# A three-stage attention and mixing kernel: unit 0's decays in two halves, and a new order of all steps

## The chip, the core and the metric

The kernel runs on one core of one Trainium2 chip. Its metric is the device time of one execution in microseconds (us): 578.5 us is the median of three runs of the kernel before (578.36 to 580.26). Five engines work side by side, each through its own list of instructions in order: TensorE (PE in the rows, PEld for its loads of weights), VectorE (DVE), ScalarE (ACT), GpSimd (POOL) and SyncE (SP). ACT, POOL and SP also issue DMAs.

## The reference

Three stages, for batch 4, 8 heads, 768 tokens, 48 channels a head (384 in all):

```python
# 1: linear attention with a decay per channel and token
for t in range(S):
    state = alpha[:, :, t, :, None] * state + np.einsum('bhd,bhe->bhde', k[:, :, t], v[:, :, t])
    y[:, :, t] = np.einsum('bhd,bhde->bhe', q[:, :, t], state)
...
# 2: mixing over tokens with a phase, then over channels
theta = x @ w_theta
zr, zi = x * np.cos(theta), x * np.sin(theta)
u = x + np.einsum('ts,bsd->btd', w_tok_r, zr) + np.einsum('ts,bsd->btd', w_tok_i, zi)
x = u + np.maximum(u @ w_ch, 0.0)
...
# 3: a gated layer with a second mixing over tokens
h = np.maximum(x @ w_in, 0.0)
u, v = h[..., :512], h[..., 512:]
v_n = (v - mu) / np.sqrt(var + 1e-06)
out = (u * (np.einsum('ts,bsd->btd', w_spatial, v_n) + b_spatial[None, :, None])) @ w_out
```

## The kernel before, in words

The work of stages 1 and 2 is cut into 24 units: 4 sequences of 6 blocks of 128 tokens. A unit u goes through these steps, named by the functions that issue them:

- `load_al`, `load_qk`, `load_v` (L360, L370, L375) load its decays, its queries and keys, and its values.
- `att_scan` (L380, L388, L391, VectorE) turns the decays into running products: a scan backward over 8 groups of 66 numbers, a reciprocal of 8 numbers, and a scan forward. `att_qk` (L414) multiplies queries and keys by them.
- TensorE takes over: `att_k` (L463) transposes keys, `att_u` (L480) makes the state's increments, `att_a` (L428) the scores, `att_y` (L527) the outputs; from unit 6 on one step, `att_uya` (L602), does most of this for two units. VectorE masks the scores (`att_mask`, L435) and carries the state on (`att_s`, L495, and `att_t`, L508).
- `tr_p` (L634), `th_p` (L674, L677) and ScalarE's and VectorE's steps between them make the phase; `z_m` (L716, L712 for unit 0), `z_h` (L720) and `z_l` (L724) the two products that are mixed over tokens; `tokmix` (L750) adds them into five banks of PSUM, which hold one sequence. After the sixth unit `evac` (L774) empties the banks and `ch_p` (L802) mixes channels.

Stage 3 (L926 to L1160) follows per sequence, its first products already beside the last units.

The weights come in 28 pieces, 22 of them packed. A packed piece is loaded by `raw_f64` (L247; GpSimd issues the first 16), unpacked by `top` (L253, ScalarE) and `join` (L262, VectorE), and split into two parts by `high` (L273, ScalarE) and `low` (L281, VectorE); unit 0's pair is multiplied whole before it is split. The raw pieces share 2 buffers, `top` and `join` share one tile (zeros), and the joined pieces one (f); a piece's load waits until the `join` two pieces earlier has read its buffer.

Fourteen products named `fill` (L761, 2 instructions each) multiply a tile of zeros into one of the five banks before the first `tokmix` adds to it. They need only the small tile of constants (`cst_sb`) and the zeroed tile `heads`, so they can stand anywhere ahead of it.

What sets the order: the functions declare about 1700 steps, and `ORDER`, a table of numbers written into the kernel, says in which order they are issued. Each engine gets its own instructions in that order and waits for others by semaphores. Tiles come from pools that go round: 2 buffers for decays (al), 3 for queries and keys (qk), 2 for values (vd). A load waits on its issuing engine until the step that read the buffer last is done, and what stands behind it on that engine waits too.

The constant AH decides on unit 0's decays. With AH = 0, `load_al` and `att_scan` handle all 8 groups of unit 0 at once. With AH = 1, `load_al` takes groups 0 to 3 and a further step `load_ah` (L365) groups 4 to 7, and `att_half` scans the first four before `att_scan` scans the others:

```python
n = 4 * SEG if AH and u == 0 else 8 * SEG
issuer("load_al", u).dma_start(t[:, :n], al_in[u, :, :n])
...
def att_half(u):
    scans(u, 0, 4, "bif")
...
def att_scan(u):
    if AH and u == 0:
        scans(u, 4, 8, "bif")
    else:
        scans(u, 0, 8, "f" if u in RP else "bif")
```

Of the kernel before, what the change touches and what calls it, by code (L numbers as in the profile page):

```python
# [75 lines left out]
AH = 0  # L76
# [13 lines left out]
1 130 167 177 131 67 0 175 7 132 178 176 179 133 180 68 134 69 181 12 138 139 70 140 8 71 135 141 9 214 142 215 10 2 165 137 188 136 13 185 11 143 14  # L90
186 217 187 17 144 182 145 172 146 170 189 168 183 3 169 190 184 251 191 192 252 148 4 216 174 218 253 5 37 173 171 193 164 6 18 222 225 149 254 223
147 166 150 194 151 219 195 19 196 224 152 22 198 255 155 153 197 154 260 220 38 199 156 163 261 39 200 256 221 42 40 226 159 201 23 258 227 41 202
289 229 228 257 161 24 259 263 25 27 292 290 157 291 230 204 43 262 231 26 162 232 233 264 203 44 160 265 77 45 234 327 266 328 15 205 235 28 46 236
206 301 267 29 237 158 293 32 268 30 207 78 269 31 271 212 270 238 273 79 239 272 80 47 330 298 20 208 299 240 294 241 213 33 296 295 16 81 297 300
274 302 209 329 275 34 210 276 72 303 242 277 35 211 331 364 243 402 48 304 336 244 332 337 36 279 338 278 333 247 49 335 280 50 52 249 334 281 339
305 51 73 340 250 366 306 282 365 341 307 74 287 401 308 310 75 57 311 367 309 248 53 312 342 76 313 314 245 343 403 54 474 315 344 317 368 62 246 316
345 318 55 288 347 346 319 56 369 348 58 370 371 372 320 285 404 325 373 349 374 286 59 350 351 375 82 63 405 283 352 353 376 21 409 437 60 323 377
410 61 354 378 355 64 284 438 379 411 406 439 356 412 324 407 83 413 357 473 321 408 440 380 326 381 65 384 382 383 322 66 385 441 358 386 414 387 445
476 360 390 446 388 415 389 391 361 475 416 477 546 359 92 447 442 448 444 417 443 362 418 1009 392 421 1008 419 363 420 393 422 400 481 1010 423 394
482 449 1011 509 450 398 424 427 1012 451 425 426 84 483 399 452 510 478 512 480 395 511 396 479 453 397 454 484 455 456 1013 485 545 486 513 457 428  # L100
517 1014 429 458 1015 518 430 459 460 433 1016 548 487 431 488 514 516 515 489 519 435 490 581 520 461 521 493 462 580 522 492 463 547 436 464 87 549
494 465 1017 491 466 495 553 1018 432 496 1019 583 497 434 554 499 523 550 498 584 467 582 524 1020 555 552 551 469 556 500 616 471 1021 525 472 526
527 528 588 557 468 615 589 501 558 502 470 559 585 587 586 529 590 618 617 507 651 652 530 1022 531 532 591 533 619 560 1026 561 562 563 534 1023 535
623 508 536 1027 564 537 625 624 538 1024 88 565 1025 503 566 1028 567 543 654 568 592 505 620 593 653 626 594 627 506 655 596 687 595 622 569 504 597
570 621 688 598 571 572 659 599 660 573 544 541 600 628 601 690 602 629 661 542 724 630 656 658 662 631 663 539 657 632 723 603 634 689 633 578 664
604 691 576 605 540 606 635 607 726 574 636 695 575 696 637 577 638 1030 639 665 640 1031 641 614 727 579 610 725 666 697 692 698 694 642 667 608 669
699 1032 643 759 795 611 668 1033 670 612 1034 671 693 613 700 733 644 672 731 673 649 732 674 677 701 675 609 728 702 730 729 703 734 645 705 760 704
676 707 706 761 735 736 794 762 1035 650 708 1036 1039 678 763 679 1037 709 680 710 647 1038 713 1040 711 767 797 648 712 768 737 714 646 764 796 715
769 766 738 683 1042 765 770 739 798 684 741 740 771 743 742 829 716 830 802 1041 744 803 719 745 746 681 747 832 749 772 685 773 866 799 831 804 801
774 800 686 775 833 776 865 748 778 777 1043 682 750 779 1046 780 751 781 805 752 1044 1047 837 1045 721 838 868 782 806 839 717 807 902 783 840 722  # L110
835 784 841 842 901 808 834 1048 867 809 869 785 757 1049 786 1050 787 836 873 812 718 811 904 720 813 755 814 874 815 753 810 816 817 843 818 819 756
870 844 875 872 820 871 845 876 754 847 877 846 903 821 937 849 848 938 878 790 905 850 909 851 758 788 852 853 940 854 855 791 910 879 1053 856 789
911 880 907 792 912 906 1052 881 793 882 883 913 828 857 973 885 884 908 1054 822 941 939 1055 974 886 824 858 887 888 945 976 823 946 891 826 825 977
827 914 947 915 85 86 89 861 975 916 943 93 105 859 948 942 90 949 917 944 1056 889 862 919 918 863 890 950 920 892 1061 91 893 106 1057 1062 94 107
921 111 894 108 864 1058 922 981 923 860 982 924 927 951 925 926 109 897 978 983 928 895 929 1059 952 930 979 898 1064 110 899 1060 102 1065 1063 896
980 953 900 955 954 112 956 957 103 113 933 984 114 104 935 985 97 958 986 959 960 931 961 962 1070 987 115 1103 1068 963 98 964 1071 1066 965 1069
966 988 1067 934 989 116 990 1072 936 991 117 992 932 993 1029 967 994 95 995 969 996 96 998 971 997 999 968 118 99 1000 972 125 1001 970 1106 119
1108 1002 1107 100 1006 1109 1004 101 1051 1003 120 1007 1073 1005 1075 1110 1074 1076 1085 1077 1117 1111 1086 1094 1112 121 1091 1095 1118 1113 1124
1114 1119 1115 1116 1120 1080 1092 1125 122 1100 1126 126 1078 1101 1127 1121 1098 1081 1122 123 1123 1089 1099 1082 1090 1079 124 1087 1128 1096 1088
1104 1131 1097 1105 1129 1083 1102 127 1084 1130 128 1138 1132 129 1133 1208 1218 1154 1139 1134 1093 1228 1140 1145 1135 1141 1136 1155 1137 1152  # L120
1142 1146 1143 1147 1168 1153 1144 1148 1149 1150 1161 1151 1219 1156 1220 1222 1189 1157 1158 1229 1162 1163 1232 1233 1196 1164 1165 1223 1166 1170
1169 1167 1234 1182 1171 1172 1177 1238 1197 1239 1159 1173 1174 1175 1209 1184 1240 1178 1179 1214 1241 1180 1176 1160 1242 1185 1181 1235 1191 1243
# [13 lines left out]
1586 1587 1662 1579 1636 1588 1580 1619 1589 1581 1582 1583 1642 1590 1584 1663 1591 1615 1592 1628 1593 1616 1620 1595 1594 1621 1651 1622 1623 1596  # L136
1624 1617 1629 1625 1671 1649 1618 1626 1627 1637 1630 1638 1639 1640 1653 1631 1643 1632 1641 1633 1644 1650 1655 1645 1652 1634 1660 1646 1647 1654
1648 1669 1661 1672 1656 1664 1657 1658 1678 1659 1665 1666 1676 1667 1668 1679 1683 1677 1670 1673 1680 1674 1686 1681 1675 1684 1682 1685 1689 1687
1688 1692 1690 1691 1695 1693 1694 1698 1696 1697 1699 1700
""".split()]  # L140


# [1487 lines left out]
```

## Time and profile before

| | |
|---|---|
| median of three runs | 578.5 us (578.36 to 580.26) |
| the profiled execution | 579.89 us, its span 578.1 us |
| TensorE busy | 561.8 us, 97% of the span |
| VectorE busy | 443.5 us, 77% |
| ScalarE busy | 253.1 us, 44% |
| bytes moved by DMA | 65.74 MB, mean 114 GB/s |

The span begins with the first instruction and ends with the last; 1.8 us of the execution lie around it. Matmuls are pipelined and the ends of their rows are modelled, so a row of TensorE can look busy while it waits. A row's duration overlaps the next row's start a little on VectorE as well, so what a step costs on a full engine is read from start to start. A row of several instructions is marked x and their number; "idle before" names what ended the wait.

### The profile page before, as it was taken

To read this page: it belongs to the slowest core of one execution; us is meant where nothing else is said; L and a number is where in the kernel's file an instruction comes from. 1 tells how busy PE (TensorE), PEld (TensorE's weight loads), DVE (VectorE), ACT (ScalarE), POOL (GpSimd) and SP (SyncE) were. 2 spreads that over 40 slices of the span, in tenths; PEclk is the share of its full clock that TensorE was granted. 3 is DMA by queue.
4 is the path that set the end of the run, shared out by engine and by line. 5 is a ranking of instruction groups with operands and counts; after the bars stand their busy time and mean duration, and the time that the engine had idled before them with its cause. 6 is when DMAs were issued, how large, how long until landed. Compare 5 with 4: busy or idle time off the path is not lost.

```text
span 578.1 us, 13520 instructions
## 1 busy us (share of the span) xinstructions
PE 561.8 (97%) x5765; PEld 518.0 (90%) x5765; DVE 443.5 (77%) x785; ACT 253.1 (44%) x474; POOL 27.2 (5%) x62
## 2 busy tenths in 40 slices
PE   4998999999999999999999999999999999999997
PEld 3866888899999999999999899998999999989997
DVE  7979999998788698789656877678666685577470
ACT  3576765435434444335465433344424341344122
POOL 1111100000000000000000110000000110001000
PEclk9999999999999999999999999999999999999999
DMA  7966774527343425424256343001103010201002
GB/s 259 336 223 227 245 242 141 169 69 238 105 135 100 130 58 176 128 88 112 87 161 203 140 146 128 1 0 42 42 1 101 23 42 1 96 28 41 1 1 82
DMA packets 27739, 65.74 MB, mean 114 GB/s; under 512 B 2976, under 2 KB 13856, under 8 KB 27424
## 3 DMA queue, kind: packets, MB, share of 16 engines
q1 hardware_dynamic: 25216, 52.65, 27.8%
q0 software_dynamic: 2176, 11.86, 6.0%
q8 instruction: 45, 0.74, 0.5%
q10 hardware_dynamic: 288, 0.37, 0.2%
q14 instruction: 14, 0.11, 0.1%
HBM read 52.68 MB, written 9.44 MB: 107 GB/s over the span
## 4 chain that ended last, share of the span: by engine, by line
PE 80%; DVE 8%; issue 2%; ACT 0%; DVEq 0%; ACTq 0%
PE acc L750 20%; PE acc L1079 11%; PE psv L938 9%; PE po L1137 9%; PE pu L1011 9%; PE psc L802 6%; PE psuya L602 5%; PE sp L1050 4%; PE th L674 3%; PE th L677 1%; DVE qk L414 1%; DVE al L380 1%; PE pst L634 1%; PE psk L463 1%; DVE wf L262 1%
## 5 line engine op out<-in xcount | busy, mean ns | idle before, releaser
L750 PE MATMUL acc<-w,zs 128*128 128x384 f32 (+2 forms) x828 | 164.3, 344 | 0.5 <-DVE zs L724 0.5
L750 PEld LDWEIGHTS acc<-w,zs 128*128 128x128 f32 x828 | 132.2, 188 | 12.6 <-DVE zs L724 0.8
L1011 PE MATMUL pu<-xs,w 128*128 128x384 f32 x288 | 53.3, 336 | 0.0
L938 PE MATMUL psv<-w,xs 128*128 128x512 f32 x216 | 52.9, 394 | 0.0
L1137 PE MATMUL po<-w,gs 128*128 128x384 f32 x288 | 52.3, 336 | 0.0
L1137 PEld LDWEIGHTS po<-w,gs 128*128 128x128 f32 x288 | 50.2, 188 | 1.0 <-ACT v L949 0.3
L1011 PEld LDWEIGHTS pu<-xs,w 128*128 128x128 f32 x288 | 50.3, 188 | 0.5 <-ACT o L1147 0.2
L938 PEld LDWEIGHTS psv<-w,xs 128*128 128x128 f32 x216 | 40.2, 187 | 8.4
L1123 ACT CAST gs<-t 128x384 fp32r<-128x384 f32 x32 | 16.3, 513 | 66.2 <-DVE t L1116 66.2
L802 PE MATMUL psc<-us,wch 128*128 128x384 f32 (+1 forms) x243 | 40.8, 319 | 0.1
L802 PEld LDWEIGHTS psc<-us,wch 128*128 128x128 f32 x243 | 38.2, 189 | 0.7 <-DVE xT L812 0.4
L380 DVE TENSOR_TENSOR_SCAN al<-al,heads 112x527 f32<-112x527 f32 x24 | 30.0, 1248 | 5.4 <-DMA al<-in_al 5.4
L674 PE MATMUL th<-wth,xh 128*128 128x384 f32 x144 | 30.1, 343 | 1.9 <-DVE tmp L508 1.9
L1079 PE MATMUL acc<-w,mx 128*128 128x384 f32 x162 | 30.9, 337 | 0.0
L1079 PE MATMUL acc<-wt,vns 128*128 128x384 f32 x162 | 30.8, 336 | 0.0
L391 DVE TENSOR_TENSOR_SCAN al<-al,heads 112x527 f32<-112x527 f32 x24 | 30.1, 1256 | 0.8
L414 DVE TENSOR_TENSOR qk<-qk,al 112x1024 f32<-112x1024 f32 x24 | 29.2, 1217 | 0.1
L681 ACT ACTIVATE kk<-th,magic 128x384 f32<-128x384 f32 x24 | 14.0, 582 | 34.6 <-PE th L677 34.6
L1079 PEld LDWEIGHTS acc<-w,mx 128*128 128x128 f32 x162 | 28.5, 188 | 0.0
L1079 PEld LDWEIGHTS acc<-wt,vns 128*128 128x128 f32 x162 | 28.5, 188 | 0.0
L674 PEld LDWEIGHTS th<-wth,xh 128*128 128x128 f32 x144 | 24.9, 188 | 3.9 <-issue 2.7
L720 ACT CAST zs<-z 128x768 fp32r<-128x768 f32 x23 | 19.2, 835 | 19.4 <-DVE z L716 19.4
(126 smaller groups left out, 1051.0 us busy)
## 6 DMA issues: line engine op xcount, KB each, us to landing
qk<-in_qk SPq DMA_DIRECT2D x24, 512.0 KB, 4.5
raw<-in_w POOLq DMA_DIRECT2D x14, 772.0 KB, 5.9
vd<-in_v SPq DMA_DIRECT2D x24, 288.0 KB, 3.6
al<-in_al SPq DMA_DIRECT2D x23, 264.0 KB, 3.3
raw<-in_w SPq DMA_DIRECT2D x6, 772.0 KB, 5.6
out<-o SPq DMA_DIRECT2D x24, 192.0 KB, 1.9
x2d<-xT SPq DMA_DIRECT2D x6, 576.0 KB, 4.4
ay<-ms SPq DMA_DIRECT2D x42, 64.0 KB, 3.3
```

Of the source, the lines that this page charges most:

```text
L380: nc.vector.tensor_tensor_scan(out=rt[:, :0:-1], data0=al[:, :0:-1], data1=one[:, :0:-1], initial=1.0, op0=ALU.mult, op1=ALU.add)
L391: nc.vector.tensor_tensor_scan(out=al[:, :n], data0=al[:, :n], data1=one[:, :n], initial=1.0, op0=ALU.mult, op1=ALU.add)
L414: nc.vector.tensor_tensor(out=x, in0=x, in1=st[u]["ar"], op=ALU.mult)
L602: i = nc.tensor.matmul(ps, w, v, start=start, stop=stop)
L674: nc.tensor.matmul(th, xh[:, 0, k], wth[:, pr, k], start=(k == 0 and pr == 0), stop=False)
L750: nc.tensor.matmul(acc[b, n][:, c0:c1], zs[:, pl, ri, m * 128:(m + 1) * 128], w[:, pr, t0:t1], start=first and n != 1, stop=last, skip_gro ...
L802: nc.tensor.matmul(ps, wch[:, pl, k, m * 128:(m + 1) * 128], us[:, pr, k], start=(n == 0), stop=(n == 3 * KD - 1),)
L938: nc.tensor.matmul(ps, xs2[:, pl, k, o:o + 128], win[pr, "v"][:, k], start=(n == 0), stop=(n == 3 * KD - 1),)
L1011: nc.tensor.matmul(pu, win[f // 2][:, pl, k * 256 + f % 2 * 128:k * 256 + f % 2 * 128 + 128], xq[b, h][:, pr, k], start=(n == 0), stop=(n ...
L1050: nc.tensor.matmul(sp[:, :TH], vns[b, s][:, pl, f * 128:(f + 1) * 128], wsp[s][:, pr, t], start=(n == 0), stop=(n == 3 * NS - 1),)
L1079: nc.tensor.matmul(g, left(b, n, j, pl, c), right(n, j, pr), start=(n in (1, 5, 6) and i == 0), stop=(i == 3 * NJ - 1), skip_group_check=n ...
L1137: nc.tensor.matmul(po, gs[b][:, pl, f, s * 128:(s + 1) * 128], wo[f // 2][:, pr, f % 2 * DM:(f % 2 + 1) * DM], start=(n == 0), stop=(n == ...
```

## The change

AH goes from 0 to 1, and the table `ORDER` is replaced. There are two new steps, `load_ah` and `att_half`, both for unit 0. The number of zero products (`FILL`) is fourteen in both kernels; their places differ.

```diff
-AH = 0
+AH = 1
...
 ORDER = [int(n) for n in """
-1 130 167 177 131 67 0 175 7 132 178 176 179 133 180 68 134 69 181 12 138 139 70 140 8 71 135 141 9 214 142 215 10 2 165 137 188 136 13 185 11 143 14
...
+1 130 0 133 67 7 131 132 179 180 181 134 173 177 135 167 165 68 136 171 176 69 140 178 141 182 12 70 142 137 8 143 183 216 217 71 187 144 188 9 189
...
```

The first place is the program's start, on VectorE. Before, the scans of units 0 and 1 (L380 to L391, 527 numbers a row each), then unit 0's `att_qk`, the first `join`, and unit 1's `att_qk`:

```order
L380 SCALAR_TENSOR_TENSOR al<-al,heads 112x527
L388 RECIPROCAL al<-al 112x8
L391 SCALAR_TENSOR_TENSOR al<-al,heads 112x527
L380 SCALAR_TENSOR_TENSOR al<-al,heads 112x527
L388 RECIPROCAL al<-al 112x8
L391 SCALAR_TENSOR_TENSOR al<-al,heads 112x527
L414 TENSOR_TENSOR qk<-qk,al 112x1024
L262 SCALAR_TENSOR_TENSOR wf<-raw,zeros 128x768
L414 TENSOR_TENSOR qk<-qk,al 112x1024
L281 SCALAR_TENSOR_TENSOR w<-wf,w 128x768
```

After, two scans of 263 numbers for unit 0, its `att_qk`, the first `join`, and only then unit 1's scan:

```order
L380 SCALAR_TENSOR_TENSOR al<-al,heads 112x263
L388 RECIPROCAL al<-al 112x4
L391 SCALAR_TENSOR_TENSOR al<-al,heads 112x263
L380 SCALAR_TENSOR_TENSOR al<-al,heads 112x263
L388 RECIPROCAL al<-al 112x4
L391 SCALAR_TENSOR_TENSOR al<-al,heads 112x263
L414 TENSOR_TENSOR qk<-qk,al 112x1024
L262 SCALAR_TENSOR_TENSOR wf<-raw,zeros 128x768
L380 SCALAR_TENSOR_TENSOR al<-al,heads 112x527
L388 RECIPROCAL al<-al 112x8
L391 SCALAR_TENSOR_TENSOR al<-al,heads 112x527
L495 TENSOR_TENSOR ss<-acc_152,al 112x192
```

Unit 0's `att_qk` has moved ahead of unit 1's scan, and the first `join` too. On SyncE the load of the second half stands behind that of the first; on ScalarE the load of unit 1's decays, which stood behind that of the constants, now stands behind the loading of the activation table and one activation (L1167). On TensorE the zero products ahead of unit 0's `att_k` are six instead of three.

The second place is what VectorE has between unit 2's second `att_s` (the first row shown), which frees the buffer that unit 4's decays are loaded into, and unit 4's scan (the last row). Before:

```order
L495 TENSOR_TENSOR ss<-tmp,al 112x192
L281 SCALAR_TENSOR_TENSOR w<-wf,w 128x768
L508 TENSOR_TENSOR tmp<-acc_415,ss 112x192
L435 TENSOR_TENSOR ms<-psa,cst_sb 128x256
L262 SCALAR_TENSOR_TENSOR wf<-raw,zeros 128x768
L495 TENSOR_TENSOR ss<-tmp,al 112x192
L380 SCALAR_TENSOR_TENSOR al<-al,heads 112x527
```

After:

```order
L495 TENSOR_TENSOR ss<-tmp,al 112x192
L435 TENSOR_TENSOR ms<-acc_368,cst_sb 128x256
L508 TENSOR_TENSOR tmp<-acc_438,ss 112x192
L262 SCALAR_TENSOR_TENSOR wf<-raw,zeros 128x768
L435 TENSOR_TENSOR ms<-psa,cst_sb 128x256
L691 SCALAR_TENSOR_TENSOR r<-kk,th 128x384
L435 TENSOR_TENSOR ms<-psa,cst_sb 128x256
L281 SCALAR_TENSOR_TENSOR w<-wf,w 128x768
L495 TENSOR_TENSOR ss<-tmp,al 112x192
L262 SCALAR_TENSOR_TENSOR wf<-raw,zeros 128x768
L380 SCALAR_TENSOR_TENSOR al<-al,heads 112x527
```

Four more rows stand between them now: two masks (L435), the second `join` (L262) and unit 1's L691; the two kernels have the same VectorE steps ahead of this scan but for `att_half`. On SyncE, around the same load, before (from unit 3's decays to unit 4's queries and keys):

```order
L360 DMA al<-in_al 128x528
L370 DMA qk<-in_qk 128x1024
L375 DMA vd<-in_v 128x576 x2
L360 DMA al<-in_al 128x528
L456 DMA ay<-ms 64x256 x2
L370 DMA qk<-in_qk 128x1024
```

and after (from unit 3's values to unit 4's values):

```order
L375 DMA vd<-in_v 128x576
L360 DMA al<-in_al 128x528
L370 DMA qk<-in_qk 128x1024
L375 DMA vd<-in_v 128x576
L370 DMA qk<-in_qk 128x1024
L360 DMA al<-in_al 128x528
L456 DMA ay<-ms 64x256 x2
L375 DMA vd<-in_v 128x576
```

Unit 3's values are now loaded ahead of unit 2's, and unit 4's queries and keys ahead of unit 4's decays and of the moves of unit 3's scores (L456).

The third place is on VectorE near unit 5's `z_l` (L724), the last unit of the first sequence. The scan in these rows is unit 8's, the L495 unit 7's second `att_s`. Before:

```order
L495 TENSOR_TENSOR ss<-tmp,al 112x192
L724 TENSOR_TENSOR zs<-z,zs 128x768
L380 SCALAR_TENSOR_TENSOR al<-al,heads 112x527
L388 RECIPROCAL al<-al 112x8
L391 SCALAR_TENSOR_TENSOR al<-al,heads 112x527
L659 TENSOR_TENSOR xh<-pst,xh 128x384
L281 SCALAR_TENSOR_TENSOR w<-wf,w 128x768
```

After:

```order
L380 SCALAR_TENSOR_TENSOR al<-al,heads 112x527
L388 RECIPROCAL al<-al 112x8
L391 SCALAR_TENSOR_TENSOR al<-al,heads 112x527
L495 TENSOR_TENSOR ss<-tmp,al 112x192
L659 TENSOR_TENSOR xh<-pst,xh 128x384
L281 SCALAR_TENSOR_TENSOR w<-wf,w 128x768
L724 TENSOR_TENSOR zs<-z,zs 128x768
```

The same seven rows stand in another order: the scan (L380 to L391), L659 and a `low` (L281) have moved ahead of the `z_l`. The rest of the program keeps its steps, in an order that differs in many places by a few steps.

## Rows read from the trace of the kernel before

**Rows 1.** The page: busy us, share of the span and instructions by engine
```profile
PE 561.8 (97%) x5765; PEld 518.0 (90%) x5765; DVE 443.5 (77%) x785; ACT 253.1 (44%) x474; POOL 27.2 (5%) x62
```

**Rows 2.** Three stretches: length, busy us (instructions) by engine, PEclk, DMA share, GB/s
```profile
4.16:41.54 37.38, 32.85 (x517) 26.12 (x518) 32.50 (x52) 20.09 (x36) 3.70 (x7) 1.00 0.80 278
41.54:103.00 61.46, 57.91 (x858) 48.81 (x857) 60.95 (x91) 39.41 (x71) 3.90 (x9) 1.00 0.64 213
103.00:575.00 472.00, 471.09 (x4393) 443.06 (x4391) 349.30 (x638) 192.09 (x367) 17.49 (x39) 1.00 0.27 88
```

**Rows 3.** VectorE's timeline, 4 to 18 us: start, us, line, operation, idle before
```profile
4.16 1.26 DVE L380 TENSOR_TENSOR_SCAN al<-al,heads 112x527 f32<-112x527 f32 x1 [2.49 <-DMA al<-in_al]
...
6.87 1.23 DVE L380 TENSOR_TENSOR_SCAN al<-al,heads 112x527 f32<-112x527 f32 x1
...
9.55 1.20 DVE L414 TENSOR_TENSOR qk<-qk,al 112x1024 f32<-112x1024 f32 x1
10.66 0.95 DVE L262 SCALAR_TENSOR_TENSOR wf<-raw,zeros 128x768 uint32<-128x768 uint32 x1
...
14.30 0.55 DVE L262 SCALAR_TENSOR_TENSOR wf<-raw,zeros 128x384 uint32<-128x384 uint32 x1
...
17.47 0.96 DVE L262 SCALAR_TENSOR_TENSOR wf<-raw,zeros 128x768 uint32<-128x768 uint32 x1 [0.67 <-ACT zeros L253]
```

**Rows 4.** VectorE's timeline again, 33 to 42 us
```profile
33.42 0.95 DVE L262 SCALAR_TENSOR_TENSOR wf<-raw,zeros 128x768 uint32<-128x768 uint32 x1
34.29 0.42 DVE L435 TENSOR_TENSOR ms<-acc,cst_sb 128x256 f32<-128x256 f32 x1
...
34.89 0.55 DVE L691 SCALAR_TENSOR_TENSOR r<-kk,th 128x384 f32<-128x384 f32 x1
...
35.68 0.35 DVE L495 TENSOR_TENSOR ss<-tmp,al 112x192 f32<-112x192 f32 x1
...
38.28 0.35 DVE L495 TENSOR_TENSOR ss<-tmp,al 112x192 f32<-112x192 f32 x1
41.54 1.25 DVE L380 TENSOR_TENSOR_SCAN al<-al,heads 112x527 f32<-112x527 f32 x1 [2.90 <-DMA al<-in_al]
```

**Rows 5.** DMAs in flight near 1.2 us: count, KB each, us to landing
```profile
raw<-in_w POOLq DMA_DIRECT2D x1, 772.0 KB, 7.7
qk<-in_qk SPq DMA_DIRECT2D x1, 512.0 KB, 4.6
al<-in_al SPq DMA_DIRECT2D x1, 264.0 KB, 3.3
al<-in_al ACTq DMA_DIRECT2D x1, 264.0 KB, 4.9
cst_sb<-in_cst ACTq DMA_DIRECT2D x1, 96.0 KB, 3.5
```

**Rows 6.** The same view, the one load of decays near 36 us
```profile
al<-in_al SPq DMA_DIRECT2D x1, 264.0 KB, 5.5
```

**Rows 7.** The page's list of DMA issues, the stored outputs
```profile
out<-o SPq DMA_DIRECT2D x24, 192.0 KB, 1.9
```

**Rows 8.** ScalarE's timeline, the first 10 us
```profile
1.67 1.28 ACT L1167 ACT_TABLE_LOAD   x1 [1.67 <-PEq L1619]
...
9.23 1.06 ACT L253 ACTIVATE zeros<-raw 128x768 f16<-128x768 bf16 x1 [6.07 <-DMA raw<-in_w]
```

**Rows 9.** GpSimd's timeline, near 35 us
```profile
34.67 0.53 POOL L247 DMA_DIRECT2D raw<-in_w  x1 [3.61 <-DVE wf L262]
```

**Rows 10.** TensorE's timeline, three places in the first 100 us
```profile
4.39 2.90 PE L761 MATMUL acc<-heads,cst_sb 112*128 112x256 f32 x6 [4.39 <-DMA cst_sb<-in_cst]
21.32 1.89 PE L761 MATMUL acc<-heads,cst_sb 112*128 112x256 f32 x8
97.10 1.08 PE L750 MATMUL acc<-w,zs 128*128 128x512 f32 x5
```

**Rows 11.** VectorE's timeline, near 92 us
```profile
92.01 0.95 DVE L724 TENSOR_TENSOR zs<-z,zs 128x768 fp32r<-128x768 f32 x1
```

98 rows, old and new, of the table ORDER are left out of this document.

## The prediction

> **What bounds the kernel now.** I read the page's busy shares first: TensorE is busy for 97% of the span [rows 1], so a gain must come from the little time in which it is not. The windows say where that is [rows 2]. From 103 to 575 us TensorE is busy 471.09 of 472.00 us, and nothing is to be had there. From 4.16 to 41.54 us it misses 4.5 us, and to 103 us another 3.6. Before 4.16 us nothing runs on it.
>
> The second number to read in those windows is VectorE's. From 41.54 to 103 us it is busy 60.95 of 61.46 us: no gap at all. Everything that TensorE multiplies in this time (scanned decays, masks, products, split weights) passes through VectorE, so the end of this stretch is where VectorE began it plus the work. From its first scan at 4.16 us to unit 4's scan at 41.54 us, VectorE is idle 37.38 - 32.50 = 4.88 us [rows 2], and 2.90 of these are one wait, for unit 4's decays [rows 4]. So I count in VectorE's time: when it starts, what is added to its list, and how long it waits, up to unit 4's scan. The work ahead of that scan is the same in both orders, but for the half scan. What is won there I carry to the end one for one, because VectorE is full from there to 103 us and TensorE from there on.
>
> **The change, part by part.**
>
> *Start.* Unit 0's whole decays (264 KB) landed 3.3 us after their issue [rows 5], and the scan began at 4.16 us [rows 3], so the issue is near 0.8 us. No row shows a load of 132 KB at the start. The nearest ones are the stored outputs, 192 KB in 1.9 us [rows 7], and the constants, 96 KB in 3.5 us beside the first decays [rows 5]; so the scan may begin between 2.7 and 4.3 us. I take a landing in 2.7 us, between the two and nearer to the row of the same tensor: start at 3.5, -0.65 us (bounds -1.5 and +0.1).
>
> The Trainium skill bears on this ("DMA: Bandwidth & Descriptors", Anatomy of one DMA): a DMA that GpSimd issues costs about 2.0 us fixed plus its bytes at 436 GB/s, so half the bytes save little. This load goes by SyncE; with that rule's slope, 132 KB less would be an estimated 0.31 us, a start at 3.85, and a sum 0.35 us higher than mine; no run here shows it.
>
> *Two halves.* A whole scan takes 6.87 - 4.16 = 2.71 us on VectorE [rows 3]. The halves have three more instructions. A join of 384 numbers takes 0.55 us and one of 768 takes 0.95 [rows 3], so 0.15 us of each instruction does not depend on its length; two of these, and a reciprocal with its gap, 2.71 less twice 1.26, 0.2 us, make +0.5 us (bounds +0.2, the reciprocal alone, and +0.8, a quarter microsecond for each of the three).
>
> *The first join.* After the halves VectorE is at 3.5 + 2.71 + 0.5 = 6.7 us. Unit 0's queries (4.6 us from an issue near 1.2 us [rows 5]) are there, so `att_qk` runs from 6.7 to 7.8 us, 1.11 us from start to start [rows 3] and 2.85 us earlier than before. Next on VectorE now stands the first `join`, which needs `top` (L253). That ran from 9.23 to 10.29 us, as soon as its raw piece had landed [rows 8]. Before, unit 1's scan filled this time; now it is queued behind the `join`, and with it units 0 and 1's `att_s`. The piece took 7.7 us [rows 5], with unit 1's decays in flight ahead of it. These are now issued after the table load, so 264 KB less stand ahead of the piece; at the stretch's mean of 278 GB/s [rows 2] that would be 0.95 us, less if more is moved at the start, when many loads are in flight. I take 0.7 us, the `join` at 9.6 instead of 10.3: +1.8 us of waiting (bounds 0, if the piece comes as fast as unit 1's decays did, in 4.9 us [rows 5], and +2.5, if nothing is gained for it).
>
> *Unit 1's decays.* They are issued about 1.5 us later, after the table load of 1.28 us and the activation behind it [rows 8], near 2.8 us. With their own 4.9 us they land at 7.7, with the raw piece's 7.7 at 10.5. They are wanted at 9.6 + 0.87 = 10.5 us. I take 0 (bounds 0 and +1.9, if unit 1's queries, 512 KB at the same mean rate, go first as well).
>
> *The other small waits.* 4.88 - 2.90 = 1.98 us, the longest 0.67 us, for `top` of the third piece [rows 3]. That `join` now stands behind unit 2's scan, 2.71 us later in the list, and needs no wait; the others have been moved apart in the same manner. I take -1.6 us (bounds -1.98 and 0).
>
> *Unit 4's decays.* Before, their buffer came free at 36.03 us (35.68 + 0.35), they landed 5.5 us after their issue [rows 6], and VectorE, which had work until 38.63 us, waited 2.90 us [rows 4]. Ahead of them on the DMA engines was the 772 KB of a raw piece issued at 34.67 us [rows 9], which waited for the `join` at 33.42. The new order puts that very `join` and three short rows between: 0.87 (33.42 to 34.29), two masks of about 0.34 and L691's 0.47 [rows 4], 2.0 us more of cover, 4.6 in all. And since the raw piece's load waits for that `join`, it is now issued after the decays. With 5.5 us, 0.9 us of waiting would stay; with 3.3 [rows 5], none. I take -2.6 us (bounds -2.9 and 0, if the queries of unit 4, 512 KB, which are now ahead on SyncE, take the raw piece's place).
>
> *Values of units 2 and 3* change places on SyncE. Unit 2's now wait for unit 1's `att_y`, and unit 4's queries and decays are queued behind them. That step stands ahead of unit 2's masks in both orders, and those ahead of the `att_s` that frees unit 4's decays: nothing, with VectorE's work between as the cover.
>
> *Zero products.* Fourteen either way. Six of them, twelve instructions at the 0.48 us of the first ones (2.90 us for six [rows 10]), keep TensorE from 4.39 to 10.2 us, while unit 0's `att_k` is ready at 7.8. But VectorE wants what follows from it only behind unit 1's scan, at 9.6 + 0.87 + 2.71 = 13.2 us; the 3.0 us between cover two short products and a copy, and I cost this at nothing (up to +1 if they don't).
>
> Sum: -0.65 + 0.5 + 1.8 + 0 - 1.6 - 2.6 = -2.55 us. Against the profiled execution, 579.89 us (span 578.1 and 1.8 around it), that is 577.3 us. The median of the runs is 578.5, 1.4 us lower, so I forecast 576.0 us. All lower bounds together give -6.2, all upper ones +6.3 us.
>
> **The rivals.**
>
> *All of it.* Both groups of waits vanish (-1.98 and -2.9) and the raw piece comes a little sooner (+1.4 of waiting): -0.65 + 0.5 + 1.4 - 1.98 - 2.9 = -3.6, 574.9 us. For it: VectorE had no gap for 60 us once it was fed. Against it: a new order brings new waits, as the first `join` shows.
>
> *Given back at unit 5.* Its `z_l` ended at 92.96 us [rows 11], and its first `tokmix` began at 97.10 [rows 10]: 4.1 us to spare. Now a scan (2.71), L659 (0.47) and a `low` (0.87) stand ahead of it: 4.05 us less to spare, none left. If TensorE, which gets there with less waiting now, has to stand there or at the evacuation behind it for 1.5 us, the gain is 1.05 us and the time 577.5: no change that could be told, since about 0.3% (1.7 us) is what a measurement of this kernel resolves. The first `join` at its upper bound with unit 4's wait half kept comes to the same.
>
> *Slower: the clock.* Six instructions of zero products took 2.90 us at 4.39 us, eight took 1.89 at 21.32 [rows 10]: 0.48 and 0.24 us each, half the pace, 1.2 against 2.4 GHz, although the granted clock is listed as 1.00 in both stretches [rows 2]. Between them TensorE had pauses, then ran without one. If six products at the front leave it with more pauses later and the fast pace comes 10 us later than 21 us, 10 us of near-full work take 5 us more: -2.55 + 5 = +2.45, 581.0 us. It decides from 8.5 us of delay, half of which is the 2.55 won and the 1.7 of 0.3%. Against it: the front is busier than before, six products instead of three without a pause.
>
> **How the numbers follow.** Forecast 0.42, its own range 574.9 to 577.5; all of it 0.20; given back 0.28; slower 0.10. Of the forecast's 0.42, 0.05 lies above 576.8, where 0.3% ends. Faster: 0.37 + 0.20 + 0.02 from the edge of the third = 0.59. Same: 0.05 + 0.26 + 0.01 = 0.32. Slower: 0.09. The range leaves a tenth on each side, 573.6 to 579.6 us.
>
> **What would show it.** VectorE's first scan near 3.5 us, and rows of about 0.7 us for the halves; a wait for ScalarE (L253) of about 1.8 us before the first L262; unit 4's scan near 39 us instead of 41.54, with its wait for a load under 0.5 us; VectorE again without a gap to about 100 us; unit 5's L724 near 93 us, with the first L750 after it waiting for it little or not; TensorE's pace doubled by 21 us. Unit 4's scan at 41 us or later would make the prediction wrong, and a scan at 39 us with an end unchanged would show that VectorE's lead is not carried to the end.

## The result: slower by 0.7%, and the profile after

The changed kernel takes 583.96 us in the median of 6 runs (582.05 to 585.20), the kernel before 579.03 us on the same chip (6 runs): a ratio of 1.0071, 95% interval 1.0053 to 1.0089. (The two medians by themselves, 4.9 us apart, would give 1.0085, which lies inside the interval; 0.0071 of 579 us is 4.1 us.) The forecast was 576.0 us. The profiled execution took 583.79 us, its span is 582.0 us.

| | before | after |
|---|---|---|
| median, us | 579.03 | 583.96 |
| span of the profiled execution, us | 578.1 | 582.0 |
| unit 4's scan begins, us | 41.54 | 40.45 |
| TensorE idle from 103 to 575 us | 0.91 | 3.47 |

The page's busy shares of after and the three windows that answer to [rows 1, 2] (length; busy us and instructions of PE, PEld, DVE, ACT, POOL; granted clock; DMA share; GB/s):

```profile
PE 565.3 (97%) x5765; PEld 519.9 (89%) x5765; DVE 442.7 (76%) x788; ACT 254.1 (44%) x474; POOL 26.8 (5%) x62
```
```profile
3.31:40.45 37.14, 32.30 (x476) 25.89 (x476) 32.81 (x54) 17.16 (x31) 3.17 (x6) 0.82 0.83 284
40.45:103.00 62.55, 61.09 (x904) 51.50 (x903) 61.83 (x93) 42.88 (x75) 4.43 (x10) 1.00 0.64 216
103.00:575.00 472.00, 468.53 (x4371) 439.49 (x4370) 347.38 (x637) 191.66 (x365) 17.05 (x39) 1.00 0.26 86
```

Up to unit 4's scan after is 1.1 us ahead of the profile of before. What is new lies behind: from 103 us on, where the forecast had TensorE full, it misses 3.5 us. (Of the 0.91 us before, 0.62 only stand there because TensorE was done ahead of 575 us.) The start, on VectorE (start, us, line, operation, idle before), answers to [rows 3, 4]:

```profile
3.31 0.71 DVE L380 TENSOR_TENSOR_SCAN al<-al,heads 112x263 f32<-112x263 f32 x1 [1.64 <-DMA al<-in_al]
...
6.03 0.70 DVE L391 TENSOR_TENSOR_SCAN al<-al,heads 112x263 f32<-112x263 f32 x1
9.62 1.23 DVE L414 TENSOR_TENSOR qk<-qk,al 112x1024 f32<-112x1024 f32 x1 [2.88 <-DMA qk<-in_qk]
10.91 0.96 DVE L262 SCALAR_TENSOR_TENSOR wf<-raw,zeros 128x768 uint32<-128x768 uint32 x1
11.79 1.25 DVE L380 TENSOR_TENSOR_SCAN al<-al,heads 112x527 f32<-112x527 f32 x1
...
40.45 1.26 DVE L380 TENSOR_TENSOR_SCAN al<-al,heads 112x527 f32<-112x527 f32 x1
```

The first scan, the half rows (0.7 us) and the missing wait at 40.45 us are as forecast. The wait of 2.88 us for unit 0's queries was not. The DMAs in flight in the same stretch as [rows 5] show why (count, KB each, median us to landing):

```profile
raw<-in_w POOLq DMA_DIRECT2D x1, 772.0 KB, 8.3
qk<-in_qk SPq DMA_DIRECT2D x1, 512.0 KB, 7.9
al<-in_al SPq DMA_DIRECT2D x2, 132.0 KB, 3.2
al<-in_al ACTq DMA_DIRECT2D x1, 264.0 KB, 4.0
```

The queries took 7.9 us where they took 4.6. And the place that costs most, on VectorE and then on TensorE:

```profile
175.70 0.36 DVE L495 TENSOR_TENSOR ss<-tmp,al 112x192 f32<-112x192 f32 x1
...
180.45 1.25 DVE L380 TENSOR_TENSOR_SCAN al<-al,heads 112x527 f32<-112x527 f32 x1 [2.87 <-DMA al<-in_al]
...
183.15 0.53 DVE L691 SCALAR_TENSOR_TENSOR r<-kk,th 128x384 f32<-128x384 f32 x1
183.59 1.02 DVE L774 TENSOR_TENSOR xT<-acc,xT 128x256 f32<-128x256 f32 x2
```
```profile
180.90 1.52 PE L750 MATMUL acc<-w,zs 128*128 128x384 f32 x7
184.07 1.08 PE L750 MATMUL acc<-w,zs 128*128 128x256 f32 x5 [1.65 <-DVE xT L774]
```

L495 frees the buffer of unit 16's decays, which land 4.3 us later. VectorE waits 2.87 us with their scan, the evacuation of sequence 1 (L774) is queued behind it, and TensorE's L750 waits for that evacuation. Before, the load was issued at 174.24 us, 1.8 us earlier, two products (L716, L724) stood ahead of the scan, and TensorE did not wait. VectorE's rows of before:

```profile
176.07 0.95 DVE L716 TENSOR_TENSOR z<-z,x 128x768 f32<-128x768 f32 x1
177.92 0.96 DVE L724 TENSOR_TENSOR zs<-z,zs 128x768 fp32r<-128x768 f32 x1 [0.90 <-ACT zs L720]
178.80 1.25 DVE L380 TENSOR_TENSOR_SCAN al<-al,heads 112x527 f32<-112x527 f32 x1
...
182.43 1.94 DVE L774 TENSOR_TENSOR xT<-acc,xT 128x512 f32<-128x512 f32 x4
```

### The profile page after: what moved, and what is told of

Same layout as the page of the kernel before. It is cut to its first block, busy times and chain, and to the rows that moved or that the text cites. A ratio compares the mean times of both kernels' runs of the same rounds, so it can differ in the third digit from the quotient of the medians.

```text
span 582.0 us, 13522 instructions
## 1 busy us (share of the span) xinstructions
PE 565.3 (97%) x5765; PEld 519.9 (89%) x5765; DVE 442.7 (76%) x788; ACT 254.1 (44%) x474; POOL 26.8 (5%) x62
## 4 chain that ended last, share of the span: by engine, by line
PE 81%; DVE 9%; DMA 6%; issue 2%; ACT 1%; POOL 0%; SPq 0%; DVEq 0%; POOLq 0%; ACTq 0%
PE acc L750 21%; PE acc L1079 11%; PE pu L1011 9%; PE po L1137 9%; PE psv L938 8%; PE psc L802 7%; PE psuya L602 6%; PE sp L1050 4%; DMA raw<-in_w 3%; PE th L674 3%; PE th L677 2%; DVE xT L774 1%; PE psk L463 1%; DVE wf L262 1%; DVE w L281 1%
## 5 line engine op out<-in xcount | busy, mean ns | idle before, releaser
L750 PE MATMUL acc<-w,zs 128*128 128x384 f32 (+2 forms) x828 | 166.5, 345 | 2.6 <-DVE xT L774 1.7
L750 PEld LDWEIGHTS acc<-w,zs 128*128 128x128 f32 x828 | 132.7, 188 | 15.9 <-DVE xT L774 2.0
L802 PE MATMUL psc<-us,wch 128*128 128x384 f32 (+1 forms) x243 | 41.7, 320 | 0.4 <-DVE us L790 0.3
L802 PEld LDWEIGHTS psc<-us,wch 128*128 128x128 f32 x243 | 38.2, 189 | 1.7 <-DVE us L790 0.5
L380 DVE TENSOR_TENSOR_SCAN al<-al,heads 112x527 f32<-112x527 f32 (+1 forms) x25 | 30.2, 1207 | 5.5 <-DMA al<-in_al 5.4
L391 DVE TENSOR_TENSOR_SCAN al<-al,heads 112x527 f32<-112x527 f32 (+1 forms) x25 | 30.3, 1212 | 0.9
L674 PE MATMUL th<-wth,xh 128*128 128x384 f32 x144 | 30.0, 343 | 0.7 <-DVE ms L435 0.5
L253 ACT ACTIVATE zeros<-raw 128x768 f16<-128x768 bf16 (+1 forms) x22 | 23.0, 1045 | 13.8 <-DMA raw<-in_w 13.4
L674 PEld LDWEIGHTS th<-wth,xh 128*128 128x128 f32 x144 | 24.7, 188 | 3.1 <-ACT xh L641 1.2
## 6 DMA issues: line engine op xcount, KB each, us to landing
x2d<-xT SPq DMA_DIRECT2D x6, 576.0 KB, 4.3
```

The source lines that it names most:

```text
L380: nc.vector.tensor_tensor_scan(out=rt[:, :0:-1], data0=al[:, :0:-1], data1=one[:, :0:-1], initial=1.0, op0=ALU.mult, op1=ALU.add)
L391: nc.vector.tensor_tensor_scan(out=al[:, :n], data0=al[:, :n], data1=one[:, :n], initial=1.0, op0=ALU.mult, op1=ALU.add)
L674: nc.tensor.matmul(th, xh[:, 0, k], wth[:, pr, k], start=(k == 0 and pr == 0), stop=False)
L750: nc.tensor.matmul(acc[b, n][:, c0:c1], zs[:, pl, ri, m * 128:(m + 1) * 128], w[:, pr, t0:t1], start=first and n != 1, stop=last, skip_gro ...
L802: nc.tensor.matmul(ps, wch[:, pl, k, m * 128:(m + 1) * 128], us[:, pr, k], start=(n == 0), stop=(n == 3 * KD - 1),)
```

## Experiments

Two theories at first. Theory 1: the time is lost in the new order behind the start, at places like this one. Theory 2: it is lost in the start (halves, late queries, the clock). Ratios are to the kernel before on the same chip, with the 95% interval in brackets; two kernels ran once, for their profile.

### Which part of the order: two hybrids

The two orders have done the same steps at step 290 (bar one each), so they can be exchanged there. OTHER is the other kernel's list.

```diff
-        for key in (keys[n] for n in ORDER):
+        first = ORDER[:292]      # 290 in the reverse one, with before's list as ORDER
+        for key in (keys[n] for n in first + [n for n in OTHER if n not in first]):
```

> The changed kernel's first 292 steps (to unit 6's att_a, which TensorE reaches at 77.12 us in the profile of the changed kernel and at 78.53 us before), then every other step in the order of before. Theory 1, the time is lost in the new order behind this place: the lead of 1.41 us is kept, 579.0 - 1.4 = 577.6 us, ratio 0.9976, with no stand of TensorE near 182 us. Rival (theory 2), the start costs it (halves, late queries of unit 0, clock at half until 25.5 us): 583 us or more, ratio over 1.005.

> The reverse: the first 290 steps of before (whole scan of unit 0, no halves), then every other step in the changed kernel's order. Theory 1: the losses of the later order without the lead of the start, 584.0 + 1.4 = 585.4 us, ratio 1.011. Theory 2: 579.0 us as before, ratio 1.000.

Measured: the changed start with the order of before 579.09 us, ratio 1.0010 (0.9984 to 1.0036); the start of before with the changed order 584.82 us, 1.0090 (1.0058 to 1.0123). The loss comes with the later order, and theory 2 falls. But the first hybrid is not at 577.6 either: the lead of 1.41 us at step 290 did not show. It was a lead over one execution. A second profile of the kernel before (below) has TensorE at unit 6's `att_a`, the place of the exchange, ahead of the changed kernel; first that profile, then the changed kernel:

```profile
76.14 0.69 PE L428 MATMUL psa<-qk 48*64 48x64 f32 x32
```
```profile
77.12 0.69 PE L428 MATMUL psa<-qk 48*64 48x64 f32 x32
```

From this step to the end of the span it is 499.1 to 500.7 us in all nine profiles here with the order of before behind it, those with a changed start included. With the changed order behind it, it is 504.9 us in the changed kernel and 503.4 to 507.1 in the four others in which at most one thing of it is changed; the second hybrid, which gets to the step first of all (76.06 us), has the 507.1. So the loss is made behind this step, whatever the start. TensorE's waits from 160 to 275 us (waiter, releaser: us in total, times, longest), first with the start of before and the changed order, then in the changed kernel; the kernel before has no line in this stretch:

```profile
PE acc L750 <- DVE xT L774: 1.8, 1, 1.8
PE th L677 <- DVE xh L659: 0.2, 1, 0.2
PE acc L750 <- DVE acc L769: 0.2, 1, 0.2
```
```profile
PE acc L750 <- DVE xT L774: 1.7, 1, 1.7
PE th L677 <- DVE xh L659: 0.2, 1, 0.2
PE acc L750 <- DVE acc L769: 0.2, 1, 0.2
```

The same stand in both, whatever the start.

### The stand at 182 us

The edits from here on use one helper, put in ahead of the last loop:

```diff
+        def behind(place, *names):     # move steps behind another
+            for name in names:
+                order.remove(name)
+            n = order.index(place) + 1
+            order[n:n] = names
```

First try, the cover:

```diff
+        behind(("att_qk", 15), ("z_m", 12), ("z_h", 12), ("z_l", 12))
```

> The changed kernel with three steps of unit 12 (z_m, z_h, z_l) moved behind att_qk of unit 15, where before has z_m and z_l, so that att_s of unit 14 comes 1.8 us earlier, the load of unit 16's decays too, and two products of 0.9 us cover it. Theory 1: VectorE's wait of 2.87 us ahead of unit 16's scan falls under 0.5 us, TensorE's stands of 2.0 and 0.3 us at 182 to 187 us go, 584.0 - 2.3 = 581.7 us, ratio 1.0046. Rival (theory 3), something else ends last there (the evacuation's own 4 us, or the accumulators): the wait goes and TensorE stands for another, 584 us, ratio 1.008 to 1.009.

Measured 584.28 us, 1.0090 (1.0057 to 1.0122): nothing won, and my expectation failed at its first step (an earlier `att_s`). VectorE's wait for the decays is gone, but `att_s` of unit 14 came no earlier (176.2 us): it waits for TensorE, not for the products moved away from it, so VectorE now stood 0.72 and 1.32 us ahead of it instead, and 0.95 us between the two products. The scan began at 180.79 us, TensorE waited 1.50 us for L774. Second try, the dependency:

```diff
+        behind(("tokmix", 11, 0, 1), ("evac", 1, 1))
```

> The changed kernel with one step of the list exchanged: sequence 1's evac of part 1 (it reads columns 256 to 511 of accumulator 1) stands behind the last tokmix of part 0 (it adds to columns 0 to 255 of the same accumulator), as before has it, not ahead. No engine's own order changes; only who waits for whom. Theory 1a, TensorE's 1.7 us at 182 us is this dependency: L750 no longer waits for VectorE's L774, att_uy of unit 14 begins at 183 instead of 185 us although VectorE still waits 2.9 us for the decays; some of it comes back as a wait for the zeroed accumulator (L769) at 187 us, so 584.0 - 1.3 = 582.7 us, ratio 1.005 to 1.006. Rival (theory 3): the time comes back whole, as TensorE's wait for L769, and the end is unchanged, 584.0 us.

Third, with two more places:

```diff
+        behind(("tokmix", 11, 0, 1), ("evac", 1, 1))
+        behind(("evac", 1, 0), ("acc_zero", 2))
+        behind(("att_scan", 22), ("evac", 2, 1))
```

> The same, and two more places: the zeroing of accumulator 1 for sequence 2 directly behind its evacuation, and sequence 2's evac of part 1 directly behind unit 22's scan, ahead of the masks and of the last tokmix of part 0 (as before has it), where VectorE waited 1.17 us for it at 262 us. Theory 1: TensorE's stands at 182 to 187 us (2.3 us) and at 262 to 267 us (1.2 us) go, and the end comes with them, 584.0 - 3.5 = 580.5 us, ratio 1.0025; TensorE busy 40.0 of 40 us from 160 to 200 and from 240 to 280 us. Rival (theory 3): TensorE's stands move on, ratio 1.006 or more.

Measured: 583.08 us, 1.0077 (1.0056 to 1.0098), and 580.86 us, 1.0033 (1.0018 to 1.0049). The first moves no instruction on any engine; it only lets the last products of part 0 go ahead of the evacuation of part 1, with which they share an accumulator. VectorE still waits 2.87 us, TensorE no longer. Its row at the place of 184.07 us:

```profile
180.56 2.35 PE L750 MATMUL acc<-w,zs 128*128 128x384 f32 x12
...
185.39 1.31 PE L750 MATMUL acc<-w,zs 128*128 128x384 f32 x6
...
187.18 1.09 PE L750 MATMUL acc<-w,zs 128*128 128x256 f32 x5 [0.48 <-DVE acc L769]
```

By the time it can't be told from the changed kernel. The profiled span, 580.7 us, is 1.3 us shorter, as much as I expected, but the changed kernel's own six spans go from 580.3 to 583.4, so what this one edit gives at the end is not shown. With all three edits the view of TensorE's waits from 160 to 275 us has no line left, and the windows that held the stands are full (160 to 190 and 255 to 270 us; before the edits 28.27 and 14.51):

```profile
160.00:190.00 30.00, 29.98 (x494) 27.24 (x484) 25.61 (x46) 13.53 (x28) 0.30 (x3) 1.00 0.41 127
255.00:270.00 15.00, 15.00 (x206) 13.69 (x204) 14.55 (x26) 6.43 (x13) 0.10 (x1) 1.00 0.28 91
```

By the medians, 584.0 - 580.9 = 3.1 us of the 4.9 lost are these two ends of sequences; by the ratios, 1.0071 to 1.0033, it is 2.2 of 4.1. From unit 6's `att_a` to the end the third kernel takes 501.6 us. So half of the loss or more is made there: theory 1 holds, and theory 3 falls.

### Why the queries land late

```diff
+        order.insert(order.index(("load_al", 0)) + 1, ("load_ah", 0))      # on the order of before
+        order.insert(order.index(("att_scan", 0)), ("att_half", 0))
```

> The order of before, with unit 0's decays loaded and scanned in two halves and nothing else changed. Theory 1: the start comes 0.85 us earlier (3.31 for 4.16 us) and the halves take 0.7 us more (3.42 us from 3.31 to 6.73, for 2.71), unit 1's scan follows them at once, and the queries of unit 0 are not wanted before 9.4 us: 579.0 us, within 0.3 us, ratio 1.000. Theory 2, the halves themselves cost time (unit 0's queries or unit 1's decays land later behind the two loads): 580.5 us or more, ratio 1.003 or more.

```diff
+        behind(("load_v", 0), ("load_qk", 0))                              # on the order of before
```

> The kernel before with one exchange on SyncE: unit 0's queries are issued behind its values, at 1.66 us instead of 1.20, so behind the first raw piece's issue at 1.42; no halves. Theory 4: the queries land 7 us or more after their issue instead of 4.3 to 4.6. Rival (theory 5), the two half loads themselves delay them: under 5.5 us. The time should not move by more than 1 us: they are wanted at 9.5 us. The page also shows once more how long VectorE waits for unit 4's decays in the order of before: 2.9 us if the profile of before is typical, 0.9 to 1.1 us if the first and second experiments' are.

```diff
+        behind(("load_al", 0), ("load_qk", 0))                             # on the first hybrid
+        behind(("att_qk", 0), ("att_scan", 1))
```

> The kernel of the first experiment (the changed start, then the order of before) with two steps exchanged: unit 0's queries issued ahead of the second half of its decays, and unit 1's scan ahead of the first join. Theory 4, the queries land late because they are issued 0.47 us later, behind the first raw piece: they land 4.3 to 4.9 us after an issue at 1.2 instead of 7.9 after 1.66, att_qk of unit 0 begins near 7 instead of 9.6 us, VectorE is 2.5 us further at the first join, unit 4's scan stands near 38 instead of 40.0 us. On the end: if VectorE's lead at unit 4 is carried on, 579.1 - 2 = 577 us, ratio 0.9975; if it is not (unit 5's scan and the end are set by other things), 579 us, ratio 1.000. On the clock: with no pause of TensorE at 9 us it is granted in full from 8.4 us on.

Measured: halves alone 579.60 us, 1.0005 (0.9979 to 1.0030), no change, and so no gain; queries behind the values 577.70 us in one execution; queries first 580.95 us, 1.0023 (1.0007 to 1.0039). The queries' row in the three, in this order:

```profile
qk<-in_qk SPq DMA_DIRECT2D x1, 512.0 KB, 7.3
```
```profile
qk<-in_qk SPq DMA_DIRECT2D x1, 512.0 KB, 7.4
```
```profile
qk<-in_qk SPq DMA_DIRECT2D x1, 512.0 KB, 4.4
```

Theory 5 falls, the halves have no part in it: issued at 1.66 us the queries take 7.2 to 8.4 us in every profile here, with halves or without, and issued at 1.20 us 4.3 to 4.6. GpSimd issues the first raw piece (772 KB) at 1.42 us, in between. Issued behind it, the queries land with it: in the nine profiles 0.2 to 0.8 us ahead of the `top` (L253) that waits for the piece. The bytes ahead of them on SyncE's own queue are the same 264 KB with halves as without. No run moves the piece alone, so that it and nothing else holds them up is argued, not shown. The Trainium skill ("DMA: Bandwidth & Descriptors", Queues, rings and completion order) says that each DMA engine goes round between the queues packet by packet; by that alone I would estimate that 0.46 us of delay cost the queries about as much. The runs show 3 us, and what makes up the rest stays open.

Theory 4 holds for the order of issue, but what I built on it did not follow. In the third kernel VectorE reaches unit 1's scan 2.4 us earlier (9.10 us for 11.47 in the first hybrid; 0.9 of these are the `join`, which now stands behind it) and unit 4's 1.2 us later (41.26 for 40.04): it waited 1.37 us for ScalarE at 23.8 us, 1.12 at 32.2, and 0.90 for TensorE at 35.3. So the lead was gone within 30 us.

### The clock

In the changed kernel's start six zero products run at 3.5 to 8.8 us, TensorE then stands, and the granted clock, listed as 1.00 until 11.8 us, is 0.50 (1.2 GHz) until 25.5 us; in the third kernel above until 32 us. With the order of before the pace is doubled from 21 us at the latest [rows 10].

```diff
+        behind(("att_a", 0), ("fill", 0))
+        behind(("tr_p", 0), *[("fill", n) for n in (6, 11, 13, 10)])
+        behind(("att_y", 1), *[("fill", n) for n in (3, 7, 9, 5)])
+        behind(("th_p", 0, 0), ("fill", 1))
+        behind(("th_p", 1, 1), ("fill", 4))
```

> The kernel of the seventh experiment with the zero products laid as before has them: three ahead of unit 0's att_k instead of six, four behind tr_p of unit 0, four behind att_y of unit 1. Theory 6, the clock: six products at the front raise TensorE's granted clock at 8 us, it falls back to half in the pause behind them (at 12 to 15 us) and is full again only at 22 to 31 us; with three it is not granted and lost, and comes at 20 us as before. Then VectorE's waits for ScalarE and TensorE between 23 and 36 us (1.4, 1.1, 0.9 us) shrink, unit 4's scan stands near 38.5 instead of 41.3 us, and the end follows, 580.9 - 2.4 = 578.5 us, ratio 0.999. Rival (theory 7), the order of the start itself, not the clock, holds VectorE back there: unit 4's scan over 40.5 us and 580 us or more.

> The changed kernel with the zero products alone laid as before has them. Theory 6: granted clock full from 20 us instead of 25.5, unit 4's scan at 39.5 instead of 40.45 us, 584.0 - 1 = 583 us, ratio 1.007 (1.0071 was measured for the changed kernel, so 1.005 to 1.006). Rival (theory 7): no change in VectorE's times, 584 us.

Measured: 579.88 us, 1.0009 (0.9994 to 1.0025), and 583.44 us, 1.0069 (1.0047 to 1.0092). The clock did as expected. From 20 to 24 us, the changed kernel and then the same with three products first (the last figures are granted clock, DMA share, GB/s):

```profile
20.00:24.00 4.00, 4.00 (x43) 3.42 (x40) 3.93 (x9) 0.54 (x2) 0.53 (x1) 0.50 0.81 262
```
```profile
20.00:24.00 4.00, 4.00 (x77) 3.80 (x70) 3.93 (x7) 0.56 (x3) 0.00 (x0) 1.00 0.81 271
```

TensorE does 77 instructions for 43, and VectorE, busy 3.93 of 4.00 us in both, gains nothing: from unit 2's scan to unit 4's it takes 20.99 us for 21.31. The expected scan at 39.5 us came at 41.04, that of the other kernel (38.5) at 42.25; in its profiled execution the second half scan began 1.8 us later than in the kernel it is compared with, and from unit 2's scan to unit 4's it took 22.78 us for 23.94. That is 0.3 and 1.2 us less. But the same stretch took 20.92 to 22.27 us in five other profiles that have the changed start and its zero products unmoved, so a price of half speed is not shown; if there is one, it is about 1 us or less. The medians say no more: 0.5 us less than the changed kernel and 1.1 less than the third kernel, with intervals that overlap. Theory 6, which forecast 1.0 and 2.4 us, is not borne out. With the clock as before, unit 4's scan is still at 41.04 us, for 39.16 in the second profile of before, so most of what holds the changed start back is its order, as theory 7 says.

### Unit 4's decays, and whether a lead is carried

> The kernel before, unchanged, profiled a second time. Theory 11, the wait of 2.90 us for unit 4's decays belongs to the one execution that was profiled: now 0.4 to 1.3 us, unit 4's scan at 39.1 to 39.7 us, span 575.5 to 576.5 us. Rival: the wait is the kernel's, 2.5 us or more.

Theory 8 says that a lead at unit 4 is carried to the end; the kernel before is asked first. Profiled once more, it took 577.33 us, span 575.6. Its row at unit 4's scan, the one that answers to 41.54 us in [rows 4]:

```profile
39.16 1.26 DVE L380 TENSOR_TENSOR_SCAN al<-al,heads 112x527 f32<-112x527 f32 x1 [0.34 <-DMA al<-in_al]
```

0.34 us, not 2.90 (0.4 to 1.3 expected). Theory 11 holds: the wait on which my largest term rests belonged to one execution, in which the decays took 5.5 us to land; in the three others with that stretch unchanged they took 3.0 to 3.6 and the wait was 0.46 to 1.06 us.

```diff
+        behind(("att_t", 2, 0), ("att_s", 2, 1))                           # both on the order of before
+        behind(("att_s", 2, 1), ("load_al", 4))
```

> The kernel before with one step moved: att_s of unit 2 that frees unit 4's decays stands two rows earlier on VectorE, ahead of th_r of unit 1 and a mask, so the load is issued about 1.2 us earlier. In four executions with the order of before VectorE waited 2.90, 0.88, 1.06 and 0.46 us for these decays. If a lead at unit 4 is carried to the end (theory 8: unit 4's scan at 39.2 to 39.3 us went with spans of 575.4 and 575.9 us, at 41.5 us with 578.1), the wait goes and the median falls by what is typical of it, 0.5 to 1.0 us: 578.3 us, ratio 0.998 to 0.999. Rival: nothing to be seen, since the wait of 2.9 us belongs to one execution and another wait takes its place, ratio 1.000.

```diff
+        behind(("att_t", 2, 0), ("att_s", 2, 1))
+        behind(("att_s", 2, 1), ("load_al", 4), ("join", 7), ("raw_f64", 8), ("high", 7))
+        behind(("att_mask", 3, 0), ("low", 7))
```

> The kernel before with what the new order does at unit 4's decays and nothing else of it: att_s of unit 2 and the decays' load ahead of the join whose end lets GpSimd issue the next raw piece (772 KB), so that the piece is issued behind the decays and not 0.7 to 2.2 us ahead. Theory 9, in the order of before the decays land at 39.0 to 39.6 us whenever they are issued (35.0 to 36.2 us), or at 41.5, because the piece goes first; behind them it costs them nothing: they land 3.1 to 3.4 us after an issue near 34.4 us, VectorE does not wait, unit 4's scan stands at 38.3 us, 0.9 to 1.4 us earlier than in the other runs with this order, and the end follows: 578.0 us, ratio 0.998. Rival: the piece's own join is late instead, or the end does not follow, ratio 1.000.

Measured: 578.17 us, 0.9988 (0.9973 to 1.0002), and 578.04 us, 0.9989 (0.9976 to 1.0002). Neither is faster than before beyond doubt, and no other kernel here is. In the first the decays were issued at 35.04 us, 0.6 us or more ahead of the others, and landed 4.6 us later, no earlier than there; VectorE waited 1.30 us. In this run and the four others with the raw piece ahead, the profile of rows 6 aside, the decays landed 0.6 to 1.0 us behind the piece, however long behind it they were issued. In the second, issued ahead of the raw piece, they landed 2.7 us after 34.23 us, and VectorE did not wait for them: so far theory 9 holds. Its gain went into another wait ahead of the same scan:

```profile
37.06 0.56 DVE L691 SCALAR_TENSOR_TENSOR r<-kk,th 128x384 f32<-128x384 f32 x1 [1.76 <-ACT kk L681]
...
40.65 1.25 DVE L380 TENSOR_TENSOR_SCAN al<-al,heads 112x527 f32<-112x527 f32 x1
```

TensorE had stood 2.46 us there, to 32.1 us, and its granted clock was 0.50 from 32 to 35 us, the only such dip with that order. Whether the move brings this stand or one execution did is open. Theory 8 holds over the kernels that follow the order of before throughout: unit 4's scan at 39.16, 39.19, 39.31, 39.70, 40.65 and 41.54 us goes with spans of 575.6, 575.9, 575.4, 576.0, 577.9 and 578.1 us. 2.4 us at the scan are 2.5 us at the end. It holds for the three hybrids with a changed start too (40.04, 41.26 and 42.25 us go with 577.1, 577.5 and 578.9): from the scan to the end it is 536.1 to 537.3 us in all nine, and 541.6 in the changed kernel.

### The other places put back

```diff
+        behind(("att_qk", 7), ("th_r", 5))                                 # beside the three of the sixth experiment
+        behind(("acc_zero", 1), ("att_mask", 8, 0), ("move_a", 8))
+        behind(("ch_l", 3, 0), ("low", 19))
```

> The kernel of the sixth experiment with three more places put back: unit 7's att_qk ahead of unit 5's th_r (84 us), unit 8's first mask and its move behind the zeroing for sequence 1 (104 to 109 us), and weight piece 19's low behind the residual split of the last sequence (330 us). Theory 1 carried through, all that is lost is lost at such places: 0.4 + 0.5 + 0.6 us less than the sixth experiment, 580.9 - 1.5 = 579.4 us, ratio 1.0005 to 1.001. Rival (theory 10), the rest of the loss is in the start: 580.5 us or more, ratio 1.003.

Measured 582.75 us, 1.0069 (1.0042 to 1.0096): 1.9 us slower than without these three by the medians, with intervals that just overlap; the expectation of 579.4 us failed. From unit 6's `att_a` to the end it is 503.8 us, for 501.6. TensorE is busy 18.27 of 20 us from 100 to 120 us (19.37 without them) and 33.70 of 35 from 310 to 345 us (34.57). What I moved aside was wanted there, by L674 and L802:

```profile
PE th L674 <- DVE xh L659: 1.1, 1, 1.1
PE psc L802 <- DVE xT L812: 1.0, 1, 1.0
```

So it does not tell where the last 1.8 us (1.9 by the ratio) are; that stays open. The sixth experiment's windows point to the same stretches, 19.53 of 20 us from 80 to 100, 19.37 to 120 and 34.57 of 35 to 345 us, where the second profile of before has 25.81 of 26 us from 77 to 103 and no wait of TensorE to 160 us.

## Why the prediction was wrong, point by point

- *Start, two halves.* Right in size: the scan at 3.31 us (3.5 forecast), half rows of 0.7 us, the end of the halves at 6.73 us (6.7). But what the early start wins was again read against one profile: with whole decays the first scan begins at 3.66 to 3.77 us in the five other executions, so 0.3 to 0.5 us and not 0.65 were to be had, no more than the halves cost (+0.5 forecast, 0.71 in the changed kernel).
- *The first join.* The time was nearly right (10.91 us, 9.6 forecast, 10.66 before) and the reason wrong. "Unit 0's queries (4.6 us from an issue near 1.2 us) are there" is the failed sentence: the second half's issue puts theirs 0.47 us later, behind the raw piece's, and they land at 9.6 us. The wait ahead of `att_qk` was 2.88 us, for a DMA; the 1.8 us of waiting for ScalarE did not come. I counted the halves' instructions on VectorE and not the one that they add on SyncE.
- *Unit 1's decays.* Wrong, without a price: they are issued at 1.24 us, while the table load runs, and landed 4.0 us later.
- *The other small waits* (-1.6 us). Too large: VectorE is idle 37.14 - 32.81 = 4.33 us up to unit 4's scan; without the 2.88 for the queries 1.45 stay, 0.93 of them one wait for ScalarE at 25.2 us, where 1.98 were before.
- *Unit 4's decays* (-2.6 us). The mechanism was right: no wait ahead of the scan at 40.45 us. The size was one execution's: a second profile of before has 0.34 us. Set against that one, unit 4's scan is 1.3 us later in the changed kernel (40.45 for 39.16), where I had it 2.55 earlier than before.
- *Zero products, the clock rival.* The fast pace came later, as the rival says, by 5 us and not 10. Laid as before, they gain nothing that can be told from the scatter, as forecast, and VectorE is the one that is full there.
- **The step that failed: "What is won there I carry to the end one for one, because VectorE is full from there to 103 us and TensorE from there on."** Carrying holds for one order behind unit 4, as nine spans show. But the change is another order to its last step, and I priced it only up to unit 5, as if it kept TensorE full from 103 us on because the old one did. It does not: from unit 4's scan to the end it takes 5.0 us more (541.6 for 536.6), and TensorE is idle 3.47 us from 103 to 575 us for 0.91. Of the 4.9 us lost, 3.1 by the medians (2.2 of 4.1 by the ratios) are shown at two ends of sequences by the sixth experiment, and where the rest is lost stays open. At those two places the new order names an evacuation ahead of a product that adds to the same accumulator, or behind one that it need not wait for. The rival "given back at unit 5" looked for this kind of loss in one place, and unit 5's `z_l` (95.33 us, 92.01 in [rows 11]) made TensorE wait 0.2 us.

## What to carry to other kernels

When a list of 1,700 steps is replaced, the profile of before vouches for no stretch of it: look through the new order, to the end of the kernel, for a load's wait with other work queued behind it, and for an evacuation whose place among the products of a shared accumulator has changed. A wait for a DMA in one profile is a sample, and so is every lead that is read against that profile: here -2.6 us of the forecast and the lead of 1.41 us at step 290 were one execution's. Look at a second profile before it becomes the largest term. And an added DMA is priced by what it pushes back on its own queue.

## What the runs showed of the hardware that was not expected

- 0.46 us of issue time went with 3 us of landing: 512 KB issued at 1.20 us, ahead of GpSimd's 772 KB at 1.42, landed in 4.3 to 4.6 us; at 1.66 us, behind it, in 7.2 to 8.4, with the larger load.
- The same load in the same order took 5.5, 3.4, 3.6, 3.0 and 2.9 us to land in five executions, and the wait behind it was 2.90, 0.88, 1.06, 0.46 and 0.34 us.
- ScalarE's queue issued a DMA at 1.24 us beside a table load that ran from 1.18 to 2.46 us.
- A step's place in the list, with every engine's own order unchanged, took away a wait of 1.65 us on TensorE.
